# Slot-read rows put on the partitions slot by slot instead of batch by batch

## The chip, the cores and the metric

One core of a Trainium2 chip. The metric is device time in microseconds (us) of one execution; lower is better. A profile of a run gives a "span", from the first to the last instruction, which is about 2.1 us less than the device time of the same run.

Some words used below. TensorE (PE in the profile) does the matmuls, VectorE (DVE), ScalarE (ACT) and GpSimd (POOL) the other computations; SyncE (SP) issues copies, and in runs 4 to 7 ScalarE or GpSimd do so too. SBUF and PSUM are on-chip memories of 128 rows, called partitions; matmuls write to PSUM. A DMA is a copy between memories, here from SBUF to the output in DRAM; it is cut into packets, which the core's 16 DMA engines carry. Its instruction *issues* it; it has *landed* at the last update of its semaphore, the counter by which a waiting engine knows that the copy is complete. An *eviction* takes matmul sums out of PSUM.

## The reference

A cross attention between tokens `x` and a small state, in both directions, then a two-layer network with a squared relu on all rows. The output has, for each of 8 batches, 512 token rows and 32 "slot-read" rows (what the 32 state slots read from the tokens).

```python
# B, H, S, Ns, D = 8, 8, 512, 32, 64
a     = softmax(x @ state.T / sqrt(D));   xread = a  @ state      # 512 rows per batch
a2    = softmax(state @ x.T / sqrt(D));   sread = a2 @ x          #  32 rows per batch
rows  = concat([xread, sread], axis=2)    # -> (B * 544, H * D)
h     = rows @ w_in                       # 512 -> 2048
g     = s * relu(h) ** 2 + b
out   = g @ w_out                         # (4352, 512), float32
```

## The kernel before

The token rows go through the network batch by batch. The 8 x 32 = 256 slot-read rows ("sr") go through it together, last of all. `h` holds 128 hidden units on the partitions and the 256 rows as columns, batch by batch: column = 32 * batch + slot. The relu on ScalarE moves it from PSUM to SBUF.

```python
def relu(name, f, ntok):
    def fn(e):
        ...
        if e == "DVE":
            nc.vector.tensor_scalar(g_of(name, f), OSB["h", name, f], 0.0, None, ALU.max)
        else:
            nc.scalar.activation(g_of(name, f), OSB["h", name, f], AF.Relu)
```

For the second layer the 256 columns are taken as two halves of 128 rows (batches 0 to 3 and 4 to 7), and so are the output columns. Seven steps of matmuls on sums of halves give four output quarters of 128 rows x 256 columns. The order of the rows inside a half is free, as long as both halves have the same order. In the second layer, a column of `g` becomes an output partition.

```python
STEPS = [(0, 4, 4, True, False), (1, 6, 6, True, True), ...]         # 7 steps; cut
PUT = {1: ("c11", 0, 0), 4: ("c22", 1, 1), 5: ("c12", 0, 1), 6: ("c21", 1, 0)}   # step: quarter, row half, column half

def step_put(b, n):
    def fn(e):
        name, rows, h = PUT[n]
        if b == "sr":
            dst = out_BSn[4 * rows : 4 * rows + 4, S:ST, hD * h : hD * h + hD]   # 4 batches x 32 slots x 256
            ENG[e].dma_start(dst, SN[b, name][:, 0])                             # from 128 partitions x 256
            return
        ...                                                                      # the token rows, 256 rows of 1 KB
```

So a slot-read output DMA moves 128 rows of 256 fp32 (1 KB each, 128 KB in all). Its source pattern is 128 x 256 and its destination pattern 4 x 32 x 256. All four are issued from SyncE.

The softmax here doesn't subtract the row's maximum and nothing guards it: scores larger than these inputs give would overflow.

Of the kernel before, what the change touches and what calls it, by code (L numbers as in the profile page):

```python
# [156 lines left out]
def kernel(  # L157
# [13 lines left out]
    nc = tc.nc  # L171
    AF = mybir.ActivationFunctionType
    ALU = mybir.AluOpType

    B, H, S, D = x.shape
# [113 lines left out]
    G, PD, U, SN, OSB = {}, {}, {}, {}, {}  # L289
# [16 lines left out]
    ENG = {"DVE": nc.vector, "ACT": nc.scalar, "POOL": nc.gpsimd, "SP": nc.sync}  # L306
# [98 lines left out]
    for n, it in enumerate(seq):  # L405
# [5 lines left out]
        elif it[0] == "x":  # L411
            b = it[1]
# [24 lines left out]
    for k in range(8):  # L437
        b, i = 6 + k // 4, k % 4
# [324 lines left out]
    def g_of(name, f):  # L763
        return G[name, f // 4][:, f % 4, :]

    def relu(name, f, ntok):
        def fn(e):
            if (name, f // 4) not in G:
                G[name, f // 4] = gpool.tile([P, 4, ntok], FP16, name=f"g_{name}_{f // 4}", tag="g")
            if e == "DVE":  # L770
                nc.vector.tensor_scalar(g_of(name, f), OSB["h", name, f], 0.0, None, ALU.max)
            else:
                nc.scalar.activation(g_of(name, f), OSB["h", name, f], AF.Relu)  # L773

        return fn
# [246 lines left out]
    def step_put(b, n):  # L1022
        def fn(e):
            name, rows, h = PUT[n]
            if b == "sr":
                dst = out_BSn[4 * rows : 4 * rows + 4, S:ST, hD * h : hD * h + hD]
                ENG[e].dma_start(dst, SN[b, name][:, 0])
                return
            dst = out_BSn[b, 0:S].rearrange("(q c) n -> q c n", c=SCH)
            ENG[e].dma_start(dst[:, rows:SCH:2, hD * h : hD * h + hD], SN[b, name])  # L1030

        return fn
# [19 lines left out]
    for b in [*range(1, B), "sr"]:  # L1052
        nb = B if b == "sr" else b
        for n in range(7):
# [3 lines left out]
            for i in range(NKF // 2):  # L1058
                j = i // 2
# [13 lines left out]
            name = TAKE[n][0] if n in TAKE else GIVE[n]  # L1073
# [50 lines left out]
```

## Time and profile before

| | before |
|---|---|
| device time | 217.06 us, median of 3 runs (216.99 to 217.11) |
| span of the profiled run | 215.0 us |
| TensorE busy | 204.7 us, 95% of the span |
| last matmul starts | 208.39 us |
| last slot-read output: issued, landed | 209.21 us, 214.05 us |

First the page of the kernel before: the span, TensorE's row of the busy table (us, share of the span, instructions), and rows of the view in 40 slices of 5.4 us (busy share of TensorE and mean busy share of the 16 DMA engines, in tenths), with the packet count.

```profile
span 215.0 us, 4963 instructions
...
PE 204.7 (95%) x1976; PEld 132.6 (62%) x1976; DVE 176.0 (82%) x412; ACT 132.5 (62%) x288; POOL 37.3 (17%) x60
...
PE   5998999999999999999999999999999999999980
...
DMA  6999999999379996453164203311232011210221
...
DMA packets 41415, 24.05 MB, mean 112 GB/s; under 512 B 25776, under 2 KB 39600, under 8 KB 41392
```

The reader is to see a TensorE that is busy from the second slice to the second last, and idle in the last one. All that a change at the end can win lies there.

Next the chain that ended last, from 208 us (start us, us, what). "osr" is the second layer of the slot-read rows.

```profile
208.68 0.02 issue
208.70 0.48 DVE c_sr L1018
```

The chain stops at the last eviction, which ends at 209.18 us. Yet the span goes on to 215.0. The chain doesn't hold those 5.8 us, so their cause has to be looked for elsewhere. It is in what SyncE does: its timeline (start us, us from the first of a group to the end of the last, count), then its waits (us in total, times, longest).

```profile
203.37 0.53 SPq L1030 DMA_DIRECT2D out_dram<-c  x1
204.85 4.90 SPq L1027 DMA_DIRECT2D out_dram<-c_sr  x4
```

```profile
SPq L1119 <- DMA out_dram<-c_sr: 3.8, 3, 1.5
SPq L1027 <- DVE c_sr L1018: 3.2, 4, 1.9
```

The four slot-read outputs are issued between 204.85 and 209.75 us (one by one: at 204.85, 207.47, 208.34 and 209.21), each when its eviction is done. After that, SyncE waits 3.8 us for three of them to land. Now the windows of the tail: each line is one stretch (us from the span's start) with its length and the busy time of each engine, and the DMA share and GB/s are the last two columns.

```profile
core 0: us, PE busy (x) PEld busy (x) DVE busy (x) ACT busy (x) POOL busy (x), PEclk, DMA share, GB/s
204.85:208.50 3.65, 3.65 (x35) 3.16 (x33) 1.94 (x4) 0.00 (x0) 0.00 (x0) 1.00 0.26 83
...
209.30:210.30 1.00, 0.00 (x0) 0.00 (x0) 0.00 (x0) 0.00 (x0) 0.00 (x0) 1.00 0.27 90
210.30:211.30 1.00, 0.00 (x0) 0.00 (x0) 0.00 (x0) 0.00 (x0) 0.00 (x0) 1.00 0.25 65
211.30:212.30 1.00, 0.00 (x0) 0.00 (x0) 0.00 (x0) 0.00 (x0) 0.00 (x0) 0.82 0.28 93
212.30:213.30 1.00, 0.00 (x0) 0.00 (x0) 0.00 (x0) 0.00 (x0) 0.00 (x0) 0.50 0.26 87
213.30:214.30 1.00, 0.00 (x0) 0.00 (x0) 0.00 (x0) 0.00 (x0) 0.00 (x0) 0.50 0.09 31
```

From 209.3 to 213.3 us the DMA share is 0.25 to 0.28 of 16 engines, without a gap: four engines' worth, at 65 to 93 GB/s. The packet records of the trace agree. Between 208.7 and 213.7 us there are 3 to 5 packets of 1 KB in flight for 98% of the time, 4.1 on the mean (4 for two thirds of the time).

The relu of the slot-read rows is cheap and short (line, engine, output<-input, count | busy us, mean ns | idle before it, releaser):

```profile
L773 ACT ACTIVATE g_sr<-h_sr 128x256 f16<-128x256 f32 x16 | 6.1, 383 | 10.5 <-PE h_sr L209 10.4
```

### The profile page before, as it was taken

To read this page: it belongs to the slowest core of one execution; us is meant where nothing else is said; L and a number is where in the kernel's file an instruction comes from. 1 tells how busy PE (TensorE), PEld (TensorE's weight loads), DVE (VectorE), ACT (ScalarE), POOL (GpSimd) and SP (SyncE) were. 2 spreads that over 40 slices of the span, in tenths; PEclk is the share of its full clock that TensorE was granted. 3 is DMA by queue.
4 is the path that set the end of the run, shared out by engine and by line. 5 is a ranking of instruction groups with operands and counts; after the bars stand their busy time and mean duration, and the time that the engine had idled before them with its cause. 6 is when DMAs were issued, how large, how long until landed. Compare 5 with 4: busy or idle time off the path is not lost.

```text
span 215.0 us, 4963 instructions
## 1 busy us (share of the span) xinstructions
PE 204.7 (95%) x1976; PEld 132.6 (62%) x1976; DVE 176.0 (82%) x412; ACT 132.5 (62%) x288; POOL 37.3 (17%) x60
## 2 busy tenths in 40 slices
PE   5998999999999999999999999999999999999980
PEld 1452334544567676667666766676667777888860
DVE  1258999999998969999999998999999988776750
ACT  4478997695385965795579558855786544532000
POOL 4923100050134261012101210121012102100000
PEclk9999999999999999999999999999999999999997
DMA  6999999999379996453164203311232011210221
GB/s 191 188 196 184 207 204 196 184 153 213 88 128 189 148 200 127 100 102 102 49 100 109 99 30 45 82 52 66 59 81 85 17 48 55 101 36 15 99 83 64
DMA packets 41415, 24.05 MB, mean 112 GB/s; under 512 B 25776, under 2 KB 39600, under 8 KB 41392
## 3 DMA queue, kind: packets, MB, share of 16 engines
q0 software_dynamic: 13840, 15.21, 35.9%
q1 hardware_dynamic: 26992, 8.40, 23.6%
q8 instruction: 15, 0.25, 0.5%
q10 hardware_dynamic: 560, 0.13, 0.3%
q14 instruction: 8, 0.07, 0.1%
HBM read 17.37 MB, written 8.91 MB: 122 GB/s over the span
## 4 chain that ended last, share of the span: by engine, by line
PE 84%; ACT 5%; DVE 5%; DMA 2%; issue 1%; SPq 0%
PE o L209 47%; PE h L209 22%; PE Mps L209 4%; PE h_sr L209 3%; PE osr L209 3%; ACT g L773 2%; DMA xf<-in_x_dram 2%; DVE g L779 1%; PE D L209 1%; ACT M L310 1%; PE V L209 1%; PE xTps L209 1%; PE T L209 1%; ACT E L540 1%; DVE u L858 1%
## 5 line engine op out<-in xcount | busy, mean ns | idle before, releaser
L773 ACT ACTIVATE g<-h 128x512 f16<-128x512 f32 x126 | 73.4, 601 | 41.5 <-PE h L209 41.3
L209 PE MATMUL h<-a,M 128*128 128x512 f16 x256 | 73.8, 380 | 0.6 <-ACT g L773 0.5
L779 DVE TENSOR_TENSOR g<-g 128x512 f16<-128x512 f16 x128 | 52.7, 420 | 3.9 <-ACT g L773 2.3
L209 PEld LDWEIGHTS <-pd 128*128 128x128 f16 x448 | 42.6, 98 | 20.0 <-issue 3.4
L209 PEld LDWEIGHTS <-g 128*128 128x128 f16 x400 | 39.0, 98 | 19.6 <-issue 0.6
L209 PE MATMUL o<-u,pd 128*128 128x256 f16 x336 | 45.9, 273 | 0.0
L209 PE MATMUL o<-wo,g 128*128 128x256 f16 (+1 forms) x288 | 45.5, 297 | 0.1
L1030 POOL DMA_DIRECT2D out_dram<-c x24 | 16.3, 679 | 103.8 <-DVE c L1018 101.0
L209 PEld LDWEIGHTS <-M 128*128 128x128 f16 x256 | 24.1, 98 | 13.2 <-issue 4.6
L310 ACT CAST M<-Mps 128x512 f16<-128x512 f32 x45 | 25.3, 595 | 7.1 <-PE Mps L209 7.1
L1018 DVE SCALAR_TENSOR_TENSOR c<-o,s_bc,bias_bc 128x512 f32<-128x512 f32 x28 | 21.0, 750 | 7.4 <-PE o L209 6.5
L795 DVE TENSOR_TENSOR pd<-g 128x1024 f16<-128x1024 f16 x28 | 19.2, 686 | 0.3
L1018 DVE SCALAR_TENSOR_TENSOR c<-o,s_bc,c 128x512 f32<-128x512 f32 x21 | 15.7, 750 | 1.8 <-PE o L209 1.6
L209 PE MATMUL o<-wo,pd 128*128 128x256 f16 x112 | 16.2, 273 | 0.0
L209 PE MATMUL o<-u,g 128*128 128x256 f16 x112 | 15.5, 273 | 0.0
L312 DVE CAST M<-Mps 128x512 f16<-128x512 f32 x19 | 13.0, 687 | 2.0 <-PE Mps L209 1.9
L773 ACT ACTIVATE g_sr<-h_sr 128x256 f16<-128x256 f32 x16 | 6.1, 383 | 10.5 <-PE h_sr L209 10.4
L540 ACT ACTIVATE E<-T 128x256 f16<-128x256 f32 x32 | 11.8, 389 | 1.1 <-PE T L209 1.1
L806 DVE TENSOR_TENSOR pd<-g,pd 128x512 f16<-128x512 f16 x28 | 11.8, 422 | 0.4
L387 POOL DMA_DIRECT2D xn<-in_x_dram x13 | 10.4, 818 | 8.6 <-DMA wi<-in_moe_w_in_dram 4.0
L804 DVE TENSOR_TENSOR pd<-g,pd 128x512 f16<-128x512 f16 x28 | 11.7, 418 | 0.0
L559 ACT ACTIVATE D<-D 128x512 f32<-128x512 f32 x16 | 9.6, 601 | 2.0 <-PE D L209 1.9
(71 smaller groups left out, 165.1 us busy)
## 6 DMA issues: line engine op xcount, KB each, us to landing
out_dram<-c POOLq DMA_DIRECT2D x24, 256.0 KB, 2.5
xn<-in_x_dram POOLq DMA_DIRECT2D x5, 512.0 KB, 22.4
wi<-in_moe_w_in_dram POOLq DMA_DIRECT2D x4, 512.0 KB, 13.2
wo<-in_moe_w_out_dram POOLq DMA_DIRECT2D x4, 512.0 KB, 18.8
xf<-in_x_dram SPq DMA_DIRECT2D x4, 256.0 KB, 3.4
out_dram<-osb POOLq DMA_DIRECT2D x4, 256.0 KB, 4.1
xn<-in_x_dram POOLq DMA_DIRECT2D x8, 128.0 KB, 4.4
out_dram<-c SPq DMA_DIRECT2D x4, 256.0 KB, 2.5
```

Source lines behind the costliest of these rows:

```text
L209: return nc.tensor.matmul(out, lhsT, rhs, start=start, stop=stop, tile_position=tp, is_transpose=is_transpose, skip_group_check=True,)
L310: nc.scalar.copy(dst, src)
L312: ENG[e].tensor_copy(dst, src)
L387: nc.gpsimd.dma_start(out=xn[b][:, h0:h1].rearrange("p h c d -> p h (c d)"), in_=x[b, h0:h1].rearrange("h (q c) d -> q h (c d)", q=P),)
L540: nc.scalar.activation(a["E"][g][:, 256 * m : 256 * m + 256], a["T"][m][:, g, :], AF.Exp, scale=scale, accum_out=a["rs"][:, g, m : m + 1],)
L773: nc.scalar.activation(g_of(name, f), OSB["h", name, f], AF.Relu)
L779: ENG[e].tensor_mul(g_of(name, f), g_of(name, f), g_of(name, f))
L795: nc.vector.tensor_tensor(pd[:, :, 0:2], g4[:, :, 1:2, :].to_broadcast((P, 2, 2, t)), g4[:, :, 0:4:3, :], ALU.subtract,)
L804: nc.vector.tensor_tensor(pd[:, :, 2], g4[:, :, 3], pd[:, :, 0], ALU.subtract)
L806: nc.vector.tensor_tensor(pd[:, :, 3], g4[:, :, 2], pd[:, :, 2], ALU.subtract)
L1018: nc.vector.scalar_tensor_tensor(t, src, s_bc, add, ALU.mult, ALU.add)
L1030: ENG[e].dma_start(dst[:, rows:SCH:2, hD * h : hD * h + hD], SN[b, name])
```

## The change

The intent: the output DMA's destination pattern should start with a dimension of 32 (slots) instead of 4 (batches). For that, partition p of a quarter has to hold slot p // 4 of batch p % 4. The change gets this by reading PSUM with a stride in the relu, which puts the columns of `g` in that order within each half.

```diff
             if e == "DVE":
                 nc.vector.tensor_scalar(g_of(name, f), OSB["h", name, f], 0.0, None, ALU.max)
+            elif name == "sr":
+                nc.scalar.activation(
+                    g_of(name, f).rearrange("p (i j b) -> p i j b", i=2, b=B // 2),
+                    OSB["h", name, f].rearrange("p (i b j) -> p i j b", i=2, b=B // 2),
+                    AF.Relu,
+                )
             else:
                 nc.scalar.activation(g_of(name, f), OSB["h", name, f], AF.Relu)
...
             if b == "sr":
                 dst = out_BSn[4 * rows : 4 * rows + 4, S:ST, hD * h : hD * h + hD]
-                ENG[e].dma_start(dst, SN[b, name][:, 0])
+                ENG[e].dma_start(dst.rearrange("b j n -> j b n"), SN[b, name][:, 0])
                 return
```

Nothing else moves: the order of instructions on the five engines is the same in both programs.

## The prediction

> **What bounds it now.** TensorE, nearly to the end: the busy table gives PE 204.7 of 215.0 us (95%), and the chain of waits is 84% PE. The change doesn't touch that part. After the last matmul (about 208.7 us in the timeline) there is a tail of 6.3 us: the last eviction, then the slot-read output DMAs.
>
> **How the tail is made.** The four slot-read output DMAs (128 KB each: 128 rows of 1 KB) are issued from SyncE at 204.85, 207.47, 208.34 and 209.21 us (timeline of SyncE's queue). The windows view shows a DMA share of 0.24 to 0.28 from 209.25 to 213.25 us, that is 4 of 16 engines, at 57 to 98 GB/s; the batch outputs just before run at a share of 0.90 and 309 GB/s. In the packet records a 1 KB packet takes 46 to 48 ns in both kinds, so one slot-read DMA is 32 packets per engine in series, 1.5 us, and the second to fourth queue behind each other from 208.67 to 213.71 us without a gap. The last lands at 214.05, and 0.91 us of closing semaphore work follow.
>
> Why 4: the Trainium skill, "DMA: Bandwidth & Descriptors", section "Why a DMA increments its semaphore by 16 and not by 1", says that the number of engines is the largest k up to 16 that divides the slowest non-1 dimension of both access patterns. Here those are 4 (batches) and 128 (partitions), so k = 4. The trace agrees (a share of 0.25). After the change they are 32 and 128, so 16.
>
> **What the change does.** The relu of the slot-read hidden rows (16 of 128x256 on ScalarE, 383 ns each) now reads PSUM with a stride, so that each half's columns, and so the output partitions, are slot by slot. The DMA's destination becomes 32x4x256. The instruction order is unchanged on all five engines; bytes and packets stay as they are.
>
> **The tail after.** Each DMA puts 8 packets on each of 16 engines: 8 x 47 ns = 0.38 us (an estimate from the packets). The last DMA no longer queues. A batch output (16 packets on each of 16 engines) took from issue at 203.37 to landing at 205.84, 2.47 us; less 8 packets, 2.09 us. So the last lands at 209.21 + 2.1 = 211.3 us in place of 214.05: 2.75 us off the span, all on the critical path, since nothing else runs then.
>
> **The relu.** If the strided read cost half again (0.6 us), it would stay hidden: the relus come every 1.1 to 1.3 us with two h buffers, ScalarE idles 0.7 to 0.9 us before most of them, and the last square (199.76 us) starts 0.5 us after its relu ends. I expect no effect on PE.
>
> **Prediction.** 217.06 - 2.75 = 214.3 us; range 213.8 to 215.0. Faster by over 2% (below 212.7): 2%; within 2%: 97%; slower: 1%.
>
> **Right or wrong in the profile.** Right: span about 212.2 us; DMA share after 209.3 us in short bursts near 0.9 rather than a level 0.25; the four issues at the same times; the last landing about 2.1 us after its issue; relu still about 383 ns; PE groups unchanged. A step is wrong if the share stays at 0.25, packets take clearly longer than 47 ns (rows of four batches interleaved), or issue takes longer than 0.54 us.
>
> **What would make it wrong.** A strided PSUM read that costs much more, delaying squares and pair sums; or a landing dominated by something other than the packets, such as a slower write receipt, which would give back part of the 2.75 us.

## The result and the profile after

| | before | after |
|---|---|---|
| device time, median | 217.09 us (216.99 to 217.13, 4 runs) | 213.99 us (213.55 to 214.26, 4 runs) |
| ratio | | 0.9856 (0.9836 to 0.9876) |
| span of the profiled run | 215.0 us | 211.7 us |
| last matmul starts | 208.39 us | 207.87 us |
| last slot-read output issued | 209.21 us | 208.69 us |
| last slot-read output landed | 214.05 us | 210.75 us |
| from last issue to last landing | 4.84 us | 2.06 us |

A ratio is the mean time of one kernel's runs over the mean of the other's in the same rounds, so it is not quite the ratio of the medians quoted here. Executions over 1.5% slower than the fastest of the same kernel are left out of the means.

The page of the changed kernel, the same rows as before:

```profile
span 211.7 us, 4963 instructions
...
PE 203.9 (96%) x1976; PEld 132.3 (62%) x1976; DVE 175.6 (83%) x412; ACT 132.6 (63%) x288; POOL 37.2 (18%) x60
...
PE   5998999999999999999999999999999999999993
...
DMA  6999999999269996573064211321132111211142
...
DMA packets 41463, 24.05 MB, mean 114 GB/s; under 512 B 25824, under 2 KB 39648, under 8 KB 41440
```

There are 48 packets more, 41463 against 41415. That is 4 DMAs x 12: each engine that takes part in a DMA writes one 4-byte packet for the completion, and each of the four DMAs now has 16 such engines in place of 4.

The end of the chain, SyncE's timeline and SyncE's waits of the changed kernel:

```profile
208.15 0.02 issue
208.18 0.48 DVE c_sr L1024
```

```profile
202.84 0.53 SPq L1036 DMA_DIRECT2D out_dram<-c  x1
204.32 4.91 SPq L1033 DMA_DIRECT2D out_dram<-c_sr  x4
```

```profile
SPq L1033 <- DVE c_sr L1024: 3.3, 4, 2.0
SPq L1125 <- DMA out_dram<-c_sr: 1.0, 2, 0.8
```

The chain again ends at the last eviction, and the four issues fill the same stretch as before (4.91 us against 4.90), only 0.52 us earlier. The closing wait for the outputs is 1.0 us in place of 3.8: this is where the time went. The windows of the changed kernel, first of the tail, then cut to the last bursts:

```profile
core 0: us, PE busy (x) PEld busy (x) DVE busy (x) ACT busy (x) POOL busy (x), PEclk, DMA share, GB/s
204.85:208.50 3.65, 3.29 (x31) 2.69 (x28) 2.09 (x5) 0.00 (x0) 0.00 (x0) 1.00 0.20 68
208.50:209.30 0.80, 0.00 (x0) 0.00 (x0) 0.16 (x1) 0.00 (x0) 0.00 (x0) 1.00 0.40 136
209.30:210.30 1.00, 0.00 (x0) 0.00 (x0) 0.00 (x0) 0.00 (x0) 0.00 (x0) 1.00 0.49 166
210.30:211.30 1.00, 0.00 (x0) 0.00 (x0) 0.00 (x0) 0.00 (x0) 0.00 (x0) 0.64 0.02 5
211.30:212.30 1.00, 0.00 (x0) 0.00 (x0) 0.00 (x0) 0.00 (x0) 0.00 (x0) 0.50 0.00 0
```

```profile
209.00:209.53 0.53, 0.00 (x0) 0.00 (x0) 0.00 (x0) 0.00 (x0) 0.00 (x0) 1.00 0.73 247
209.53:209.87 0.34, 0.00 (x0) 0.00 (x0) 0.00 (x0) 0.00 (x0) 0.00 (x0) 1.00 0.00 0
209.87:210.39 0.52, 0.00 (x0) 0.00 (x0) 0.00 (x0) 0.00 (x0) 0.00 (x0) 1.00 0.74 252
```

The level of 0.25 is gone. In its place stand bursts of 0.52 us at a share of 0.73 and 0.74 and about 250 GB/s, with nothing between them (0.00). The packets of each DMA are done before those of the next one start. The packet records show 15 to 17 packets in flight at the height of a burst, at 44 to 58 ns each. The relu with its strided read takes what it took:

```profile
L773 ACT ACTIVATE g_sr<-h_sr 128x256 f16<-128x256 f32 x16 | 6.1, 383 | 10.5 <-PE h_sr L209 10.4
```

### The profile page after: what moved, and what is told of

Its sections match the earlier page's. It is cut to its first block, busy times and chain, and to the rows that moved or that the text cites. A ratio compares the mean times of both kernels' runs of the same rounds, so it can differ in the third digit from the quotient of the medians.

```text
span 211.7 us, 4963 instructions
## 1 busy us (share of the span) xinstructions
PE 203.9 (96%) x1976; PEld 132.3 (62%) x1976; DVE 175.6 (83%) x412; ACT 132.6 (63%) x288; POOL 37.2 (18%) x60
## 2 busy tenths in 40 slices
DMA packets 41463, 24.05 MB, mean 114 GB/s; under 512 B 25824, under 2 KB 39648, under 8 KB 41440
## 4 chain that ended last, share of the span: by engine, by line
PE 90%; ACT 6%; DMA 2%; issue 0%; DVE 0%; SPq 0%
PE o L209 49%; PE h L209 25%; PE Mps L209 4%; PE h_sr L209 3%; PE osr L209 3%; ACT g L779 2%; DMA xf<-in_x_dram 2%; PE xTps L209 2%; PE D L209 2%; ACT M L310 1%; PE V L209 1%; ACT E L540 1%; PE T L209 1%; ACT D L559 1%; ACT R L566 1%
```

## The experiments

Eleven runs were made. The comparison with the reference called every one correct; run 1 shows how little this says of the order of these rows. "Issue to landing" is from the start of the last slot-read DMA instruction to the last update of its completion semaphore, both read from the trace.

| run | what | engines | issue to landing | time, median | ratio to before |
|---|---|---|---|---|---|
| before | | 4 | 4.84 us | 217.06 us | |
| changed kernel | | 16 | 2.06 us | 213.99 us | 0.9856 |
| e1_relu_only | strided relu alone | 4 | 4.92 us | 217.30 us | 1.0009 (0.9991 to 1.0027) |
| e2_dma_only | destination order alone | 16 | 2.06 us | 214.12 us | 0.9864 (0.9847 to 0.9881) |
| e3_k8 | 8 engines | 8 | 3.11 us | 214.98 us | 0.9911 (0.9895 to 0.9927) |
| e4_split | old order, 4 DMAs per quarter | 16 | see text | 214.30 us | 0.9869 (0.9850 to 0.9888) |
| e5_last4, e11_last4_b | no queue, last one on 4 | 4 | 3.36, 3.35 us | 215.53 us; 215.93 | 0.9945 (0.9920 to 0.9969) |
| e6_pool | old order, issued from GpSimd | 4, up to 8 | 4.93 us | 218.01 us | 1.0070 (1.0046 to 1.0093) |
| e7_two | changed kernel, two DMAs per quarter | 16 | see text | 214.15 us | 0.9880 (0.9858 to 0.9903) |
| e8_after | the changed kernel again | 16 | 2.06 us | 214.04 us | 0.9874 (0.9853 to 0.9896) |
| e9, e10 | the kernel before again | 4 | 5.05, 5.01 us | 217.13; 217.10 | |

The ratios compare with runs of the kernel before on the same chip in the same rounds. Its median was 216.95 us beside runs 1 to 4 216.57 beside runs 5 to 8, and 217.59 in the single run beside runs 9 to 11, so the times in the table are not to be compared with 217.06 across chips.

The theory: the gain is the number of DMA engines alone, which the pattern's slowest dimension sets. Its rivals: the relu or the new order of the rows does it (runs 1, 2, 4); the addresses written, slot by slot, suit the memory better (runs 3, 4); the time saved is the last DMA's own packets, or it is the queue of three DMAs on the same four engines (runs 5, 11); any other path of issue would do as well (run 6); and the earlier start seen in the changed kernel's profile belongs to the change (runs 8, 9, 10).

### 1. The relu alone (e1_relu_only)

```diff
-                ENG[e].dma_start(dst.rearrange("b j n -> j b n"), SN[b, name][:, 0])
+                ENG[e].dma_start(dst, SN[b, name][:, 0])      # edit of the changed kernel
```

> The strided relu alone: slot-by-slot columns, but the old destination order (4 batches, then 32 slots), so the slot-read rows land in the wrong places and the result is wrong on purpose. If the gain comes from the number of DMA engines, this is the time of before (217.1 us, within 0.3), with a DMA share of 0.25 in the tail and about 4.8 us from the last issue to the last landing. If the relu or the new order of the columns brings the gain, it is near 214.0. If the strided relu costs something, it is slower than 217.1, and its 383 ns grow.

Measured: 217.30 us, ratio 1.0009 (0.9991 to 1.0027); the relu takes 383 ns. SyncE's waits in its profile:

```profile
SPq L1125 <- DMA out_dram<-c_sr: 3.9, 3, 1.6
```

The relu and the new row order alone bring nothing and cost nothing.

The comparison called this result correct, although its rows are in the wrong places. The slot-read rows are nearly the same for all slots and batches: worked out from the reference on these inputs, the standard deviation is 6e-7 between slots and 1.6e-5 between batches, and 0.052 for the whole output. A permutation of these rows is invisible to a comparison with a tolerance. So "correct" says nothing about the row order here, for the changed kernel as well. That its order is right was argued from the index patterns above; no run shows it.

### 2. The destination order alone (e2_dma_only)

```diff
-                ENG[e].dma_start(dst, SN[b, name][:, 0])
+                ENG[e].dma_start(dst.rearrange("b j n -> j b n"), SN[b, name][:, 0])      # edit of the kernel before
```

> The new destination order alone (32 slots, then 4 batches), with the old relu; the result is wrong on purpose. If the gain comes from the number of engines, 213.6 to 214.3 us, as after, with 8 packets per engine and 2.06 us from the last issue to the last landing. If the gain needs the relu, 217.1.

Measured: 214.12 us, ratio 0.9864 (0.9847 to 0.9881), 2.06 us from issue to landing.

```profile
SPq L1119 <- DMA out_dram<-c_sr: 1.0, 2, 0.8
```

The DMA's pattern brings all of the gain. With run 1 this splits the change cleanly: the relu is there only so that the rows land in the right places.

### 3. Eight engines (e3_k8)

```diff
-                    g_of(name, f).rearrange("p (i j b) -> p i j b", i=2, b=B // 2),
-                    OSB["h", name, f].rearrange("p (i b j) -> p i j b", i=2, b=B // 2),
+                    g_of(name, f).rearrange("p (i b j) -> p i b j", i=2, b=B),
+                    OSB["h", name, f].rearrange("p (b i j) -> p i b j", i=2, b=B),
...
-                dst = out_BSn[4 * rows : 4 * rows + 4, S:ST, hD * h : hD * h + hD]
-                ENG[e].dma_start(dst.rearrange("b j n -> j b n"), SN[b, name][:, 0])
+                dst = out_BSn[:, S + 16 * rows : S + 16 * rows + 16, hD * h : hD * h + hD]
+                ENG[e].dma_start(dst, SN[b, name][:, 0])      # 8 batches x 16 slots x 256
```

> A right result with 8 engines: the halves split the 32 slots instead of the 8 batches, so a DMA writes 8 batches x 16 slots. If the number of engines is what matters: 16 packets per engine, 0.75 us per DMA, shorter than the 0.87 us between issues, so no queue is left; issue to landing of the last is 2.06 + 8 x 0.047 = 2.44 us, and the time is 0.4 us above after (214.0 to 214.7). If time went simply as 1/engines with the queue kept, it would lie halfway, near 215.7. A rival in which the order slot by slot matters (rows of four batches interleaved), and not the engines, gives 217.1, since here batches come first.

Measured: 214.98 us, 0.3 us above the expected range; 3.11 us from issue to landing in place of the expected 2.44. It lies between 4 and 16 engines, as the engine theory has it, and batches come first here, which speaks against the rival of the slot-by-slot order. But the size was wrong. The windows of this run:

```profile
208.00:209.00 1.00, 0.13 (x2) 0.00 (x0) 0.48 (x1) 0.00 (x0) 0.00 (x0) 1.00 0.39 100
209.00:210.00 1.00, 0.00 (x0) 0.00 (x0) 0.00 (x0) 0.00 (x0) 0.00 (x0) 1.00 0.43 109
210.00:211.00 1.00, 0.00 (x0) 0.00 (x0) 0.00 (x0) 0.00 (x0) 0.00 (x0) 1.00 0.50 163
```

The share is 0.39, 0.43 and 0.50, and the packet records show no gap from 208.20 to 211.45 us: a queue was left after all. One unqueued DMA took 1.015 us from its first packet to its last (205.635 to 206.650), not 0.75, which is longer than the 0.87 us between two issues. The packet records show why: the packets that start in the first 0.5 us of that DMA take 82 ns on the mean (44 packets), the later ones 46. With 4 engines it is 111 ns (17 packets) and then 46.5; with 16 engines 48 ns from the start. DMAs that wait in the queue don't escape this: three of them took 3.25 us here, 1.08 each, and 5.05 us in the kernel before, 1.68 each. Why packets are slow around the start of a DMA with fewer engines was not tested and stays open.

### 4. The old order in DMAs of one batch (e4_split)

```diff
-                ENG[e].dma_start(dst, SN[b, name][:, 0])
+                for q in range(4):
+                    (nc.sync if q % 2 else nc.scalar).dma_start(dst[q], SN[b, name][32 * q : 32 * q + 32, 0])
```

> The old relu and the old layout, right result, but each output is sent as four DMAs of one batch (32 rows of 1 KB), alternately from ScalarE's and SyncE's queues. By the engine theory each runs on 16 engines (32 divides by 16) with 2 packets per engine, and the cost is the issue: two issues per queue, so the last starts 0.55 us later than one alone, with a landing about 0.55 - 6 x 0.047 = 0.3 us later than after: 214.0 to 214.6. If the slot-by-slot order itself is what helps, it stays near 217.1.

Measured: 214.30 us, in the expected range; the last quarter's four DMAs were issued at 209.22 to 209.73 us and the last landed at 211.40. Rows stay batch by batch, the relu is the old one, and nearly the whole gain is there, because 32 rows run over 16 engines. The slot-by-slot order is not what helps; it is one way to a pattern that starts with 16 or a multiple of it. Two queues are used here instead of one, but run 2 has the gain with SyncE's alone.

### 5 and 11. Without the queue, the last DMA still on four engines (e5_last4, e11_last4_b)

```diff
-                ENG[e].dma_start(dst, SN[b, name][:, 0])
+                if n == 6:                                   # the last quarter, as before
+                    nc.sync.dma_start(dst, SN[b, name][:, 0])
+                    return
+                for q in range(4):
+                    (nc.sync if q % 2 else nc.scalar).dma_start(dst[q], SN[b, name][32 * q : 32 * q + 32, 0])
```

> Takes the queue away and keeps the slow transfer: the old layout and relu, right result; the first three slot-read outputs are sent as four DMAs of one batch each (16 engines), only the last one as in before (4 x 32 rows, 4 engines, 32 packets each). If the loss of before was partly the queue of three DMAs on the same four engines, the last now takes what the first one took in before, 3.3 us from issue to landing in place of 4.84, and the time is 215.2 to 215.8, about half of the gain. If all the loss were the last DMA's own packets, it stays near 217; if it were all queue, it comes down to about 214.2.

> The run without a queue once more, as its profile fell into an execution at a far lower clock: in a fast one the last DMA is issued at about 209 us, starts 1.2 us later without queueing, has 32 packets on each of four engines for 1.7 us, and lands 3.3 to 3.4 us after its issue.

Measured: 215.53 us as the median of five runs. A sixth execution, the profiled one, took 533.61 us: its trace has no record of a full clock for TensorE, and its last matmul starts at 526 us. It is left out of the ratio, 0.9945 (0.9920 to 0.9969). Even there the last DMA took 3.36 us from issue to landing. The run was profiled again (215.93 us, a single run of unknown state, read for its trace): issued at 209.45, packets from 210.74 to 212.46, landed at 212.80, 3.35 us from issue to landing. Its windows:

```profile
209.00:210.00 1.00, 0.00 (x0) 0.00 (x0) 0.37 (x1) 0.00 (x0) 0.00 (x0) 1.00 0.57 145
210.00:211.00 1.00, 0.00 (x0) 0.00 (x0) 0.00 (x0) 0.00 (x0) 0.00 (x0) 1.00 0.23 52
211.00:212.00 1.00, 0.00 (x0) 0.00 (x0) 0.00 (x0) 0.00 (x0) 0.00 (x0) 1.00 0.26 79
212.00:213.00 1.00, 0.00 (x0) 0.00 (x0) 0.00 (x0) 0.00 (x0) 0.00 (x0) 1.00 0.12 41
```

From 210 to 212 us one DMA runs alone at a share of 0.23 to 0.26. So of the 2.8 us, 4.84 - 3.36 = 1.5 us was the queue, and 3.36 - 2.06 = 1.3 us was the last DMA's own packets on 4 engines in place of 16. Neither alone explains the gain. The queue's part is 1.5 to 1.7 us if all four profiles of four-engine DMAs are taken (4.84 to 5.05 us). The time agrees within its interval: a ratio of 0.9945 is a gain of about 1.2 us, against 2.7 for the whole change on the same chip (run 8).

### 6. The old order, issued from GpSimd (e6_pool)

```diff
-                ENG[e].dma_start(dst, SN[b, name][:, 0])
+                nc.gpsimd.dma_start(dst, SN[b, name][:, 0])
```

> The old layout and relu, right result, but the four slot-read outputs are issued from GpSimd instead of SyncE, nothing else. If that path puts a DMA of 4 x 32 rows on four engines that differ from one DMA to the next, there is no queue: a DMA share above 0.25 where two overlap, 3.3 us or a little more from issue to landing, 215.2 to 216. If it uses all 16 engines, 214.0 to 214.5. If it uses the same four engines, 217 or more, as its issue takes 0.68 us in place of 0.54.

Measured: 218.01 us, ratio 1.0070: slower than before, with 4.93 us from issue to landing. The last branch gave the time, but not for its reason. The windows:

```profile
209.00:210.00 1.00, 0.00 (x0) 0.00 (x0) 0.05 (x1) 0.00 (x0) 0.82 (x2) 1.00 0.17 26
210.00:211.00 1.00, 0.00 (x0) 0.00 (x0) 0.00 (x0) 0.00 (x0) 0.04 (x1) 1.00 0.52 104
211.00:212.00 1.00, 0.00 (x0) 0.00 (x0) 0.00 (x0) 0.00 (x0) 0.00 (x0) 0.94 0.49 91
212.00:213.00 1.00, 0.00 (x0) 0.00 (x0) 0.00 (x0) 0.00 (x0) 0.00 (x0) 0.50 0.35 107
```

The share reaches 0.5, and the packet records show 4 packets in flight for the first DMA and about 8 while two overlap, so here the engines do differ from one DMA to the next. Yet these moved 91 to 107 GB/s, little more than the 65 to 93 that four engines move from SyncE in the kernel before. The packets are 4096 bytes on this path; their median is 159 ns, but single ones took up to 1.6 us. What holds them back was not settled. Besides, the closing work after the last landing was 1.65 us in place of 0.91.

### 7. Two DMAs at once per quarter (e7_two)

```diff
-                ENG[e].dma_start(dst.rearrange("b j n -> j b n"), SN[b, name][:, 0])
+                for q in range(2):
+                    (nc.sync if q else nc.scalar).dma_start(
+                        dst[:, 16 * q : 16 * q + 16].rearrange("b j n -> j b n"), SN[b, name][64 * q : 64 * q + 64, 0]
+                    )
```

> The changed kernel, with each slot-read output sent as two DMAs of 16 slots x 4 batches (64 rows, 16 engines, 4 packets each) from ScalarE's and SyncE's queues at the same time. If part of the 1.19 us from issue to first packet grows with the rows of a DMA (in the split run 32 rows took about 0.87 us), the last landing comes 0.1 to 0.3 us after the eviction earlier than in the changed kernel: 213.5 to 214.1 us. If that latency is fixed, it equals the changed kernel.

Measured: 214.15 us as the median of five runs, against 214.04 of the unaltered changed kernel on the same chip (run 8): no gain, as in the second branch. A sixth execution, the profiled one, took 240.67 us at a lower clock (0.857); in it the time from issue to first packet is again 1.19 us (235.36 to 236.55). The latency is not shortened by sending half of the rows. Nor did the two halves start together: the packets of ScalarE's began only at 236.83 us, 1.47 us after its issue at the same time, and it landed 2.20 us after it, SyncE's 1.95 (2.06 for the undivided one). These times are from that one slow execution. The time from issue to first packet was shorter in the split run (204.80 to 205.67 us, 0.87), whose destination has one dimension less, but that was not tried alone.

### 8 to 10. Both kernels again (e8_after, e9_before_b, e10_before_c)

No edit.

> The changed kernel again, unaltered, to size the gain against the spread of before on the same chip. If the gain is the tail alone, the mean is 2.8 us below before (ratio 0.987), and the profile shows 2.06 us from the last issue to the last landing. Both kernels should show the same spread of some 0.7 us, following when TensorE's full clock is granted in the first 11 us: a grant before 9.5 us goes with a last matmul at about 207.9 us, a later one with 208.2 to 208.6. If the change itself brought the earlier start, the ratio is below 0.985 and the grant is always early.

> The kernel before, unaltered, for a second profile: its runs spread over 1.4 us (215.96 to 217.36), those of the changed kernel over 0.7. If the spread comes from the start alone, the tail is again 4.8 to 4.9 us from last issue to last landing, and the last matmul moves with the moment at which the full clock is granted. If the four-engine transfers themselves vary, the issue-to-landing time differs by some tenths of a us from 4.84.

> The same once more: a third profile of the kernel before, with the same two readings.

Measured: the changed kernel (five runs) 214.04 us, ratio 0.9874 (0.9853 to 0.9896), last matmul at 208.21 us, 2.06 us from issue to landing. The kernel before, two single runs of unknown state, read for their traces: 217.13 and 217.10 us, last matmul at 208.22 and 208.23 us, 5.05 and 5.01 us from issue to landing.

So the start of the first profile of the changed kernel (last matmul at 207.87 us against 208.39) was chance. Where it was looked at again, both kernels have their last matmul at 208.2 us. In that first pair the difference arises before 12 us and, in a second step, at about 45 us, where neither kernel runs a changed instruction. The four-engine DMAs themselves vary, 4.84 to 5.05 us in four profiles (with run 1); the sixteen-engine ones took 2.06 us in three of three.

The rule about the full clock, as expected of run 8, came from the first six profiles: granted at 8.13 and 9.19 us (run 3, changed kernel), the last matmul starts at 207.86 and 207.87 us; granted at 10.21 to 10.91 us (before, runs 1, 2, 4), it starts at 208.21 to 208.58. It didn't hold: run 11 was granted it early, at 8.46 us, and had its last matmul late, at 208.58 us. What spreads the runs of one kernel over 0.7 us (changed: 213.55 to 214.26) and 1.6 us (before: 215.96 to 217.59, on more chips) stays open.

## Why the prediction was right

It said 214.3 us with a range of 213.8 to 215.0, and 213.99 was measured (214.04 in run 8).

- **What bounds the kernel.** Right. TensorE's stretch up to the last matmul is untouched; the gain lies in the tail behind it. SyncE's closing wait fell from 3.8 to 1.0 us.
- **Four engines, then sixteen.** Right. 4.1 packets on the mean were in flight before and 15 to 17 in a burst after, and runs 1 and 2 put all of the gain on the destination pattern. The rule taken from the Trainium skill, "DMA: Bandwidth & Descriptors", section "Why a DMA increments its semaphore by 16 and not by 1", agrees with the traces: DMAs from SyncE whose smaller outermost dimension is 4, 8 and 32 ran on 4, 8 and 16 engines. The traces also show that section's account of the semaphore: 5, 9 and 16 updates per DMA, that is one for the engines left out, if there are any, and then one per engine. Only "packets stay as they are" was not exact: their count rose by 4 x 12.
- **2.75 us off the tail.** Right: 4.84 to 2.06 us from last issue to last landing, 2.78 us. The landing was estimated from a DMA of the same trace that already ran on 16 engines, less its 8 packets (2.09 us estimated, 2.06 measured). That is why it held.
- **1.5 us for a DMA on four engines.** Too small. An unqueued one took 1.74 us from first to last packet (206.107 to 207.844), since its first packets are slow. This did no harm, as the time of before was read from the trace and not summed. It did harm in the expectation of run 3, which summed packets of 47 ns and came out 0.7 us short.
- **A share near 0.9 in bursts.** Roughly: 0.73 and 0.74 over bursts of 0.52 us. Half of such a burst is start and end: in the last one the packets in flight rise for 0.13 us, stay at 16 or 17 for 0.24 us and fall for 0.14 us.
- **No cost of the relu.** Right: 383 ns before and after, 217.30 us with the relu alone.
- **The rest.** The first measurement gave 3.10 us, 0.3 more than the tail. The first profile's earlier start accounts for such a difference, and it did not come back: run 8's means differ by 2.7 us.

No version tried beats the changed kernel.

## What to carry to other kernels

Look at the outermost dimension of a DMA's pattern on both sides: 4 there left 12 of 16 engines idle here, and a level DMA share of 0.25 with nothing else running is the sign of it. It matters where nothing hides it, as at the end of a program; the chain of waits may stop at the last computation, so compare its last entry with the end of the span. If the order of the rows is in the way, let an earlier pass permute them (free here), or split the DMA along the small dimension.

## What the Trainium skill lacked or had wrong

- "DMA: Bandwidth & Descriptors" has nothing on slow first packets when fewer engines are used: those of the first 0.5 us took 111 ns with 4 engines and 82 with 8, against 46 later, and 48 with 16.
- The same page, section "Latency and other measured facts", gives about 600 ns to the first byte from SyncE's path without saying from when. Here it was 1.19 us from the start of the issuing instruction, 0.65 us from its end (the instruction took 0.54).
- The same page, section "Why a DMA increments its semaphore by 16 and not by 1", says that from GpSimd a DMA on fewer than 16 engines takes the next engines in turn. About 8 packets in flight while two DMAs overlap agree with it (run 6), but the page doesn't say what such DMAs move: it was only 91 to 107 GB/s for two together.
- "Advanced Engine Details and Errata", section "PSUM Cachelines", warns that patterns that are not contiguous slow matmuls, and says without naming an engine that every two consecutive elements should be contiguous for best throughput. For ScalarE it didn't show here: reading fp32 from PSUM with a step of 32 elements took 383 ns for 128x256, as without.
